# Linformer attention and maxout FFN on one core: attention in four TensorE groups a batch, with projections a batch ahead and AV units in six PSUM banks

## The chip, the core and the metric

The kernel runs on one core of one Trainium2 chip. The metric is the device time of one execution in microseconds (us), lower being better. A core has TensorE (matmuls, with their weight loads on a row of their own), VectorE (DVE), ScalarE (ACT), GpSimd (POOL) and SyncE (SP, which here only issues transfers). TensorE writes to PSUM, of which there are eight banks of 128 partitions by 512 float32 values; VectorE and ScalarE read results out of it.

## The reference

Eight batches of eight heads, 1024 tokens, head dimension 64. Keys and values are first projected along the sequence from 1024 to 64 rows; then comes plain attention, and its output, heads side by side, goes through a maxout layer of three weight matrices and an output matrix.

```python
# q, k, v: (8, 8, 1024, 64)   E, F: (64, 1024)
k_proj = einsum('ks,bhsd->bhkd', E, k)
v_proj = einsum('ks,bhsd->bhkd', F, v)
scores = (q @ k_proj.transpose(0, 1, 3, 2)) / sqrt(64)
scores = scores - max(scores, axis=-1, keepdims=True)
attn = exp(scores)
attn = attn / (sum(attn, axis=-1, keepdims=True) + 1e-09)
x = (attn @ v_proj), heads side by side        # (8192, 512)
h = maximum(maximum(x @ w1, x @ w2), x @ w3)   # w1, w2, w3: (512, 768)
out = h @ w_out                                # (8192, 512), w_out: (768, 512)
```

## The kernel before

The FFN is the dense work. For each half batch (`ch`, 512 tokens) there are 18 first-layer units of four matmuls (`l1`) and, half a batch later, four output units of six (`down`). They take turns in PSUM banks 0 to 3, a ring. After each unit a counter of slots ticks, and at chosen slots a piece of the next batch's attention is put into TensorE's program between dense units. Attention uses banks 4 to 7 (`AB = 4`).

```python
def l1(b, ch, c, jt, i):
    bank = fbank()                                # next of banks 0..3
    for ct in range(NCT):                         # 4 matmuls, 128x512
        nc.tensor.matmul(out=ps[:, bank, :], lhsT=w_sb[i][...], rhs=xT[b % 2][:, ct, ch, :], ...)
    if i == 0:
        nc.scalar.copy(out=h1s[jt % 2], in_=ps[:, bank, :])
    elif i == 1:
        nc.vector.tensor_tensor(out=m12[jt % 2], in0=ps[:, bank, :], in1=h1s[jt % 2], op=ALU.max)
    else:
        nc.vector.tensor_tensor(out=hT[c % 2][:, jt, :], in0=ps[:, bank, :], in1=m12[jt % 2], op=ALU.max)

def down(b, ch, c, tt):
    bank = fbank()
    for jt in range(NJT):                         # 6 matmuls, 128x512
        nc.tensor.matmul(out=ps[:, bank, :], lhsT=hT[c % 2][:, jt, tt * P:(tt + 1) * P], rhs=wo_sb[:, jt, :], ...)
    nc.scalar.copy(out=o[:, tt, :], in_=ps[:, bank, :])
    # ... every second unit: store two of them
```

The attention of batch `b + 1`, placed into the dense work of batch `b`, is six groups on TensorE: `kv`, two of `scores`, `sums` and two of `av`. The array is split into smaller tiles for them, which work side by side: `kv` in two tiles of 128 rows by 64 columns, `scores` in eight of 32 by 64, `sums` and `av` in eight of 64 by 32.

```python
def attention(b, turn):
    i = b % NB                                    # NB = 2
    def kv():                                     # 16 matmuls, bank 4
        for si in range(SI):
            nc.tensor.matmul(out=ps[0:KP, AB, :], lhsT=eT[:, si, :], rhs=k_t[i][:, :, si, :], ...)
            nc.tensor.matmul(out=ps[KP:P, AB, :], lhsT=fT[:, si, :], rhs=v_t[i][:, :, si, :], ...)
        nc.scalar.copy(out=kp2[i][:, :, :, 0, :], in_=kv_k)
        nc.vector.tensor_copy(out=kp_[:, :, 1:], in_=...)      # three more copies of it
        turn(i)                                   # transposing DMA kp2 -> kpT, by SyncE
        nc.scalar.copy(out=vp2[i][KP:P], in_=kv_v[:, 1])
        nc.vector.tensor_copy(out=vp2[i][0:KP], in_=kv_v[:, 0])
    def scores(u):                                # 32 matmuls of 256 columns, banks 4..7
        ...  # lhsT=kpT[i], rhs=qT[i]
        for gg in range(2):
            nc.scalar.activation(out=pT[:, 2 * u + gg]..., in_=ps[:, AB:AB + 4, ...], func=AF.Exp, scale=scale)
    def quads(lhs):                               # 16 matmuls, banks 4..7
        for par in range(2):
            for hh, j, g, u in QUADS:
                nc.tensor.matmul(out=ps[j * HD:(j + 1) * HD, AB + 2 * hh + par, :], lhsT=lhs(rows, g), rhs=pT[rows, g, par, :], ...)
    def sums():
        quads(lambda rows, g: ones[rows, :])
        for u in range(2):
            nc.scalar.activation(out=lns[u], in_=ps[:, AB + 2 * u:AB + 2 * u + 2, :], func=AF.Ln)
    def recip(u):
        nc.scalar.activation(out=rinv[u], in_=lns[u], func=AF.Exp, scale=-1.0)
    def av(half):
        quads(lambda rows, g: vp2[i][rows, g, half, :])
        for u in range(2):
            nc.vector.tensor_tensor(out=xT[b % 2][:, 2 * u + half, :, :], in0=ps[:, AB + 2 * u:AB + 2 * u + 2, :],
                                    in1=rinv[u]..., op=ALU.mult)
    return [(2, kv), (10, lambda: scores(0)), (15, lambda: scores(1)), (20, sums),
            (21, lambda: recip(0)), (22, lambda: recip(1)), (25, lambda: av(0)), (30, lambda: av(1))]
```

In the first batch (`b == 0`), where the pipeline fills and batch 0's own attention is still being finished, the same pieces have slots of their own: `kv` 19, `scores` 27 and 29, `sums` 31, `recip` 32 and 33, `av` 34 and 36. The inputs of batch `b + 2` are loaded by GpSimd from slot 9 of batch `b`, once the transposing DMA has landed (`load_behind_turn`), and `q_flip` transposes its q on VectorE at slots 32 to 38.

Of the kernel before, what the change touches and what calls it, by code (L numbers as in the profile page):

```python
# [10 lines left out]
BF16 = mybir.dt.bfloat16  # L11
# [5 lines left out]
def kernel(ctx: ExitStack, tc: tile.TileContext, q, k, v, E, F, w1, w2, w3, w_out, out):  # L17
# [14 lines left out]
    def T(shape, dt, name):  # L32
        return sb.tile(shape, dt, name=name)
# [77 lines left out]
    AB = 4  # L111
    HD = D // 2

    def attention(b, turn):
        i = b % NB

        def kv():
            for si in range(SI):
                nc.tensor.matmul(out=ps[0:KP, AB, :], lhsT=eT[:, si, :], rhs=k_t[i][:, :, si, :],  # L119
                                 start=(si == 0), stop=(si == SI - 1))  # L120
                nc.tensor.matmul(out=ps[KP:P, AB, :], lhsT=fT[:, si, :], rhs=v_t[i][:, :, si, :],  # L121
                                 start=(si == 0), stop=(si == SI - 1))
            kv_k = ps[0:KP, AB, :].rearrange("p (h dd f) -> p h f dd", dd=HD, f=2)
            kv_v = ps[KP:P, AB, :].rearrange("p (g u dd f) -> p u g f dd", u=2, f=2, dd=HD)
            kp_ = kp2[i].rearrange("k h f r dd -> k (h f) r dd")
            nc.scalar.copy(out=kp2[i][:, :, :, 0, :], in_=kv_k)  # L126
            nc.vector.tensor_copy(out=kp_[:, :, 1:], in_=kp_[:, :, 0:1].to_broadcast([KP, 2 * H, 3, HD]))
            turn(i)
            nc.scalar.copy(out=vp2[i][KP:P], in_=kv_v[:, 1])
            nc.vector.tensor_copy(out=vp2[i][0:KP], in_=kv_v[:, 0])  # L130

        def scores(u):
            for gg in range(2):
                g = 2 * u + gg
                for f in range(2):
                    for r in range(4):
                        rows = slice(r * HD, (r + 1) * HD)
                        for col in range(2):
                            h = HEAD[2 * g + col]
                            nc.tensor.matmul(out=ps[col * KP:(col + 1) * KP, AB + r, gg * 256:(gg + 1) * 256],  # L140
                                             lhsT=kpT[i][rows, h, f, :],
                                             rhs=qT[i][rows, h].rearrange("p (n f) -> p n f", f=2)[:, :, f],
                                             start=(f == 0), stop=(f == 1), tile_position=(r * HD, col * KP))
            for gg in range(2):
                nc.scalar.activation(  # L145
                    out=pT[:, 2 * u + gg].rearrange("p ch (t r n) -> p r (ch t) n", t=4, r=4),
                    in_=ps[:, AB:AB + 4, gg * 256:(gg + 1) * 256].rearrange("p r (si n) -> p r si n", si=SI),
                    func=AF.Exp, scale=scale)

        def quads(lhs):  # L150
            for par in range(2):
                for hh, j, g, u in QUADS:
                    rows = slice(u * KP, (u + 1) * KP)
                    nc.tensor.matmul(out=ps[j * HD:(j + 1) * HD, AB + 2 * hh + par, :],  # L154
                                     lhsT=lhs(rows, g), rhs=pT[rows, g, par, :], start=True, stop=True,
                                     tile_position=(u * KP, j * HD))

        def sums():
            quads(lambda rows, g: ones[rows, :])
            for u in range(2):  # L160
                nc.scalar.activation(out=lns[u], in_=ps[:, AB + 2 * u:AB + 2 * u + 2, :], func=AF.Ln)  # L161

        def recip(u):
            nc.scalar.activation(out=rinv[u], in_=lns[u], func=AF.Exp, scale=-1.0)  # L164

        def av(half):
            quads(lambda rows, g: vp2[i][rows, g, half, :])
            for u in range(2):
                nc.vector.tensor_tensor(out=xT[b % 2][:, 2 * u + half, :, :], in0=ps[:, AB + 2 * u:AB + 2 * u + 2, :],  # L169
                                        in1=rinv[u].rearrange("p (c n) -> p c n", c=2), op=ALU.mult)  # L170

        return [(2, kv), (10, lambda: scores(0)), (15, lambda: scores(1)), (20, sums),
                (21, lambda: recip(0)), (22, lambda: recip(1)), (25, lambda: av(0)), (30, lambda: av(1))]

    def turn_dma(i):
        nc.sync.dma_start_transpose(out=kpT[i].rearrange("p h f k -> p (h f) k"), in_=kp2[i].rearrange("k h f r dd -> k (h f r dd)"))


    state = {"f": 0, "n": 0}
# [53 lines left out]
    def quads0(ch, bank, lhs, hhs=(0, 1)):  # L233
        for hh, j, g, u in QUADS:
            if hh not in hhs:
                continue
            rows = slice(u * KP, (u + 1) * KP)
            nc.tensor.matmul(out=ps[j * HD:(j + 1) * HD, bank + hh, :], lhsT=lhs(rows, g),  # L238
                             rhs=pT[rows, g, ch, :], start=True, stop=True, tile_position=(u * KP, j * HD))

    def k_proj0(g):
        for si in range(SI):
# [16 lines left out]
                             rhs=qT[0][rows, 4 * ch + g, :], start=True, stop=True)  # L259

    def exp0(ch, g, bank):
        nc.scalar.activation(out=pT[:, g, ch, :], in_=ps[:, bank, :], func=AF.Exp, scale=scale)
# [29 lines left out]
    def scores_up0():  # L292
        for g, bank in ((0, 4), (1, 5), (2, 6), (3, 7)):
            scores0(1, g, bank)
        for g in (0, 2):
            nc.scalar.activation(out=pT[:, g:g + 2, 1, :], in_=ps[:, 4 + g:6 + g, :], func=AF.Exp, scale=scale)

    def av_up0():
        for f, bank in enumerate((6, 4)):
# [144 lines left out]

    pend = []
    for b in range(B):
        groups = attention(b + 1, turn_dma) if b + 1 < B else []
        if b == 0:
            g1 = [g for _, g in groups]
            groups = [(9, scores_up0), (12, lambda: sums0(1, 4)), (19, g1[0]),  # L450
                      (21, lambda: q_flip(1, 0)), (22, lambda: q_flip(1, 1)), (24, lambda: q_flip(1, 2)),
                      (25, lambda: q_flip(1, 3)), (27, g1[1]), (29, g1[2]),
                      (31, g1[3]), (32, g1[4]), (33, g1[5]), (34, g1[6]), (36, g1[7])]
        slot = 0
        gi = 0

        def tick():
            nonlocal slot, gi
            slot += 1
            while gi < len(groups) and groups[gi][0] <= slot:  # L460
                groups[gi][1]()
                gi += 1
            if b == 0:
                if slot == 22:
                    load_behind_turn(2, "kvq")
                return
            if b == 1 and slot in (4, 5, 6, 7):
                q_flip(2, slot - 4)
            if b + 2 < B:
                if slot == 9:  # L470
                    load_behind_turn(b + 2)
                if slot in (32, 34, 36, 38):
                    q_flip(b + 2, slot // 2 - 16)

        for ch in range(2):
            c = 2 * b + ch
            if c == 0:
                for part in ((1, range(6), (6, 7, 0, 1, 4, 5)), (2, range(3), (2, 3, 0), q_up0), (2, range(3, 6), (1, 2, 3))):
                    for _ in l1_first(*part):
                        tick()  # L480
                state["f"] = 3
# [51 lines left out]
```

## Time and profile before

| | before |
|---|---|
| time, median of 3 runs | 399.6 us (398.9 to 399.7) |
| span of the profiled execution | 397.2 us |
| TensorE busy | 388.0 us (98%) |
| TensorE weight loads busy | 171.6 us (43%) |
| VectorE busy | 200.0 us (50%) |
| ScalarE busy | 163.7 us (41%) |
| GpSimd busy | 66.6 us (17%) |
| granted TensorE clock | full |

In the profile, PE is TensorE's matmuls, PEld its weight loads, L188 is line 188 of the kernel. A group of instructions is printed as line, engine, operation, written tile <- read tiles, shape, count, then busy time and the mean of one in ns, then the idle time ahead of them and what ended it. Matmuls overlap in the array and their ends are modelled: one dense matmul is shown as 380 ns although the next starts about 216 ns after it. The distance between two starts is therefore the number to read for TensorE, and some records are missing (1043 of 1080 on L188). The lines to know: L188 is the first layer, L212 the output layer, L119 and L121 the k and v projections, L140 the scores, L154 the sums and the AV product, L145 the exponential, L161 and L164 logarithm and reciprocal of the sums, L169 the normalisation.

The chain of work that ended last is made of these shares:

```profile
PE 91%; DMA 5%; issue 1%; ACT 1%; DVE 1%; POOL 0%; POOLq 0%; DVEq 0%
```

### The profile page before, as it was taken

Reading aid. Unit: us, or ns where it says so; the run is one execution under the profiler, and the core shown is the slowest. Engines: PE = TensorE matmul, PEld = TensorE weight load, DVE = VectorE, ACT = ScalarE, POOL = GpSimd, SP = SyncE. Lnnn points to the kernel's source line nnn. Section 1 sums busy time; section 2 is a strip of 40 time slices with the busy share of each in tenths; the row PEclk is TensorE's granted clock in tenths of the full one; section 3 lists DMA queues with packets and bytes.
Section 4 is the critical chain, followed back from the end, with each engine's and each line's share of the span. In section 5 each row is a group of like instructions: output and inputs, shape, how many; then the busy total and the mean of one; then the engine's idle time right before and its main releaser. Section 6 shows DMA issues by size and latency. Waiting matters only on the chain.

```text
span 397.2 us, 6579 instructions
## 1 busy us (share of the span) xinstructions
PE 388.0 (98%) x2686; PEld 171.6 (43%) x2736; DVE 200.0 (50%) x295; ACT 163.7 (41%) x247; POOL 66.6 (17%) x110
## 2 busy tenths in 40 slices
PE   8999999999999999999999999999999999999996
PEld 4444443444444444444444444444444444444443
DVE  3347375654862476434853367433674438433341
ACT  4414447356325632256323662346423472222222
POOL 7452131050004100050001500042000000000000
PEclk9999999999999999999999999999999999999999
DMA  8999989979115972169411991149812111101022
GB/s 222 206 209 206 205 178 203 218 115 203 56 53 101 204 173 80 28 133 206 141 53 31 186 228 62 54 82 196 174 53 76 58 54 53 55 29 77 2 106 106
DMA packets 41293, 48.39 MB, mean 122 GB/s; under 512 B 9136, under 2 KB 36272, under 8 KB 41264
## 3 DMA queue, kind: packets, MB, share of 16 engines
q0 software_dynamic: 31776, 43.52, 53.1%
q1 hardware_dynamic: 8656, 3.54, 4.5%
q10 hardware_dynamic: 832, 0.92, 0.7%
q8 instruction: 21, 0.34, 0.3%
q14 instruction: 8, 0.07, 0.1%
HBM read 57.15 MB, written 16.78 MB: 186 GB/s over the span
## 4 chain that ended last, share of the span: by engine, by line
PE 91%; DMA 5%; issue 1%; ACT 1%; DVE 1%; POOL 0%; POOLq 0%; DVEq 0%
PE ps L188 58%; PE ps L212 19%; PE ps L119 3%; PE ps L154 3%; PE ps L405 3%; DMA w_sb<-in_moe_w_dram 3%; PE ps L140 2%; DMA k_t<-in_k_dram 2%; PE ps L225 1%; PE ps L396 1%; ACT pT L145 1%; DVE xT L169 1%; PE ps L238 0%; PE ps L205 0%; PE ps L285 0%
## 5 line engine op out<-in xcount | busy, mean ns | idle before, releaser
L188 PE MATMUL ps<-xT,w_sb 128*128 128x512 bf16 x1043 | 243.9, 380 | 1.9
L188 PEld LDWEIGHTS <-w_sb 128*128 128x128 bf16 x1080 | 103.1, 98 | 130.9 <-issue 10.2
L193 DVE TENSOR_TENSOR m<-ps,h1s 128x512 f32<-128x512 f32 x90 | 62.1, 690 | 134.3 <-PE ps L188 110.6
L212 PE MATMUL ps<-wo_sb,hT 128*128 128x512 bf16 x348 | 85.0, 380 | 0.5 <-issue 0.2
L191 ACT COPY h1s<-ps 128x512 f32<-128x512 f32 x90 | 52.9, 587 | 67.6 <-PE ps L188 67.6
L214 ACT COPY o_acc<-ps 128x512 f32<-128x512 f32 x59 | 34.6, 586 | 100.6 <-PE ps L212 100.6
L195 DVE TENSOR_TENSOR hT<-ps,m 128x512 bf16<-128x512 f32 x90 | 61.7, 686 | 12.4 <-PE ps L188 5.6
L219 POOL DMA_DIRECT2D out_dram<-o_acc x28 | 15.2, 544 | 273.5 <-ACT o_acc L214 264.6
L212 PEld LDWEIGHTS <-hT 128*128 128x128 bf16 x354 | 33.5, 98 | 43.1 <-issue 4.3
L169 DVE TENSOR_TENSOR xT<-ps,rinv 128x1024 bf16<-128x1024 f32 x28 | 32.9, 1217 | 7.8 <-PE ps L154 7.8
L145 ACT ACTIVATE pT<-ps 128x1024 bf16<-128x1024 f32 x28 | 27.1, 1021 | 16.4 <-PE ps L140 16.3
L99 DVE STREAM_TRANSPOSE qT<-q_t 128x512 f32<-128x512 f32 x28 | 19.4, 695 | 0.0
L87 POOL DMA_DIRECT2D v_t<-in_v_dram x21 | 15.3, 761 | 4.1 <-DMA q_t<-in_q_dram 2.0
L161 ACT ACTIVATE lns<-ps 128x1024 f32<-128x1024 f32 x14 | 13.6, 1021 | 1.6 <-PE ps L154 1.6
L164 ACT ACTIVATE rinv<-lns 128x1024 f32<-128x1024 f32 x14 | 14.2, 1060 | 0.0
L121 PE MATMUL ps<-v_t,fT 128*64 128x512 bf16 x56 | 13.4, 383 | 0.0
L119 PE MATMUL ps<-k_t,eT 128*64 128x512 bf16 x56 | 13.4, 382 | 0.0
L87 POOL DMA_DIRECT2D q_t<-in_q_dram x14 | 10.6, 769 | 3.2 <-DMA wo_sb<-in_moe_w_out_dram 1.1
L87 POOL DMA_DIRECT2D k_t<-in_k_dram x14 | 10.6, 768 | 1.9 <-ACT o_acc L443 1.1
L405 PE MATMUL ps<-xT,w_sb 128*128 128x512 bf16 x46 | 10.6, 380 | 0.2 <-issue 0.2
L126 ACT CAST kp<-ps 64x512 bf16<-64x512 f32 x7 | 4.0, 578 | 15.9 <-PE ps L121 15.9
L306 PE MATMUL ps<-warm 128*128 128x512 bf16 x23 | 8.8, 476 | 1.5 <-DVE ones L338 1.2
(82 smaller groups left out, 155.7 us busy)
## 6 DMA issues: line engine op xcount, KB each, us to landing
out_dram<-o_acc POOLq DMA_DIRECT2D x30, 512.0 KB, 2.9
q_t<-in_q_dram POOLq DMA_DIRECT2D x15, 512.0 KB, 9.3
k_t<-in_k_dram POOLq DMA_DIRECT2D x14, 512.0 KB, 11.8
v_t<-in_v_dram POOLq DMA_DIRECT2D x18, 256.0 KB, 15.2
v_t<-in_v_dram POOLq DMA_DIRECT2D x7, 512.0 KB, 15.0
w_sb<-in_moe_w_dram POOLq DMA_DIRECT2D x4, 384.0 KB, 10.3
k_t<-in_k_dram POOLq DMA_DIRECT2D x4, 256.0 KB, 8.1
w_sb<-in_moe_w_dram POOLq DMA_DIRECT2D x4, 192.0 KB, 10.0
```

Source lines behind the costliest of these rows:

```text
L87: nc.gpsimd.dma_start(out=dst[b % NB][:, slots], in_=sv[:, heads])
L99: nc.vector.transpose(out=qT[b % NB][:, hs].bitcast(FP32).rearrange("p h n -> p (h n)"), in_=q_t[b % NB][:, hs].rearrange("p h si d -> p ( ...
L119: nc.tensor.matmul(out=ps[0:KP, AB, :], lhsT=eT[:, si, :], rhs=k_t[i][:, :, si, :], start=(si == 0), stop=(si == SI - 1))
L145: nc.scalar.activation(out=pT[:, 2 * u + gg].rearrange("p ch (t r n) -> p r (ch t) n", t=4, r=4), in_=ps[:, AB:AB + 4, gg * 256:(gg + 1) * ...
L169: nc.vector.tensor_tensor(out=xT[b % 2][:, 2 * u + half, :, :], in0=ps[:, AB + 2 * u:AB + 2 * u + 2, :], in1=rinv[u].rearrange("p (c n) -> ...
L188: nc.tensor.matmul(out=ps[:, bank, :], lhsT=w_sb[i][:, ct, jt * P:(jt + 1) * P], rhs=xT[b % 2][:, ct, ch, :], start=(ct == 0), stop=(ct == ...
L191: nc.scalar.copy(out=h1s[jt % 2], in_=ps[:, bank, :])
L193: nc.vector.tensor_tensor(out=m12[jt % 2], in0=ps[:, bank, :], in1=h1s[jt % 2], op=ALU.max)
L195: nc.vector.tensor_tensor(out=hT[c % 2][:, jt, :], in0=ps[:, bank, :], in1=m12[jt % 2], op=ALU.max)
L212: nc.tensor.matmul(out=ps[:, bank, :], lhsT=hT[c % 2][:, jt, tt * P:(tt + 1) * P], rhs=wo_sb[:, jt, :], start=(jt == 0), stop=(jt == NJT - 1))
L214: nc.scalar.copy(out=o[:, tt, :], in_=ps[:, bank, :])
L405: nc.tensor.matmul(out=ps[:, bank, :], lhsT=w_sb[i][:, ct, jt * P:(jt + 1) * P], rhs=xT[0][:, ct, 0, :], start=(ct == 0), stop=(ct == NCT ...
```

## The change

The attention of a batch is laid out anew over two batches of dense work, so that it enters TensorE's program at four places instead of six.

- The k, v projection moves one batch ahead: batch `b` computes that of `b + 2`, into a bank of the dense ring, directly before the first scores of `b + 1`. Loads move ahead with it. In the first two batches, where nothing has been projected ahead yet, it keeps places of its own.
- Sums and AV are cut by half batch (`ch`) rather than by pairs of banks. AV has four units (`f`, `ch`) of two banks. Three of them run in one go: one in a pair of ring banks, two in banks 4 to 7; this is `av3`. The fourth, `av1`, is put off into the next batch and takes a pair of ring banks there, directly before the sums of the batch after.
- For this the exponentials `pT` get two buffers and the projected values `vp2` three, and the ring becomes a list from which a pair of neighbouring banks can be taken.

Cut to its core (the old functions stand above; edits by which functions take `b` as an argument, and `pT[0]` in batch 0's own code, are left out):

```diff
-    vp2 = [T([P, NPAIR, 2, D // 2], BF16, f"vp2_{i}") for i in range(NB)]
-    pT = T([P, NPAIR, 2, 512], BF16, "pT")
+    vp2 = [T([P, NPAIR, 2, D // 2], BF16, f"vp2_{i}") for i in range(3)]
+    pT = [T([P, NPAIR, 2, 512], BF16, f"pT{i}") for i in range(2)]
...
+    def kv(b, bank=AB):
...      # the same matmuls, into `bank`; then
+        nc.scalar.copy(out=kp2[i][:, :, :, 0, :], in_=...)
+        nc.scalar.copy(out=vp2[b % 3][KP:P], in_=kv_v[:, 1])
+        nc.vector.tensor_copy(out=kp_[:, :, 1:], in_=...)
+        nc.vector.tensor_copy(out=vp2[b % 3][0:KP], in_=kv_v[:, 0])
+        nc.sync.dma_start_transpose(out=kpT[i]..., in_=kp2[i]...)
...
+    def quads(b, ch, bank, lhs):                 # 8 matmuls, two banks
+        for hh, j, g, u in QUADS:
+            nc.tensor.matmul(out=ps[j * HD:(j + 1) * HD, bank + hh, :], lhsT=lhs(rows, g),
+                             rhs=pT[b % NB][rows, g, ch, :], ...)
+    def sums(b):
+        for ch in range(2):
+            quads(b, ch, AB + 2 * ch, lambda rows, g: ones[rows, :])
+        for ch in range(2):
+            nc.scalar.activation(out=lns[ch], in_=ps[:, AB + 2 * ch:AB + 2 * ch + 2, :], func=AF.Ln)
+    def norm(b, f, ch, bank):
+        nc.vector.tensor_tensor(out=xT[b % 2][:, f::2, ch, :], in0=ps[:, bank:bank + 2, :], in1=rinv[ch]..., op=ALU.mult)
+    def av3(b):
+        lo = fpair()
+        for f, ch, bank in ((0, 0, lo), (1, 0, AB), (0, 1, AB + 2)):
+            av(b, f, ch, bank)
+        norm(b, 0, 0, lo)
+    def av1(b):
+        lo = fpair()
+        av(b, 1, 1, lo)
+        norm(b, 1, 1, lo)
+    ring = [0, 1, 2, 3]
     def fbank():
-        state["f"] = (state["f"] + 1) % 4
-        return state["f"]
+        ring.append(ring.pop(0))
+        return ring[-1]
+    def fpair():
+        for i, j in ((0, 1), (1, 2), (0, 2)):
+            x, y = ring[i], ring[j]
+            if abs(x - y) == 1:
+                ring.remove(x); ring.remove(y); ring.extend((x, y))
+                return min(x, y)
...                                              # slots, with n = b + 1
+        if b == 0:
...          # kv(1) 19, q_flip 21 to 25, load 2 22, scores 27 and 29, sums 31, recip 32 and 33 as before
+            at(35, av3, 1)
+            at(36, norm, 1, 1, 0, AB)
+            at(37, norm, 1, 0, 1, AB + 2)
+        elif b == 1:
+            at(2, kv, 2)
...          # q_flip(2) at 4 to 7
+            at(9, load_behind_turn, 3, "kvq")
+            at(8, scores, 2, 0)
+            at(11, scores, 2, 1)
+            at(15, av1, 1)
+            at(15, sums, 2)
+            at(16, recip, 0)
+            at(18, recip, 1)
...          # at 24: load k, v, q of batch 4
+            at(25, av3, 2)
+            at(26, norm, 2, 1, 0, AB)
+            at(28, norm, 2, 0, 1, AB + 2)
+            at(30, kv, 3)
...          # q_flip(3) at 32 to 38
+        elif n < B:
+            if b + 2 < B:
+                at(3, lambda: kv(b + 2, fbank()))
+            at(3, scores, n, 0)
+            at(8, scores, n, 1)
+            if b + 3 < B:
+                at(11, load_behind_turn, b + 3)
+            at(14, av1, b)
+            at(14, sums, n)
+            at(15, recip, 0)
+            at(17, recip, 1)
+            at(26, av3, n)
+            at(27, norm, n, 1, 0, AB)
+            at(29, norm, n, 0, 1, AB + 2)
...          # q_flip(b + 2) at 33 to 39
+        else:
+            at(5, av1, b)
```

The list is worked off in its order, so in `b == 1` the first scores, which stand behind the load of slot 9, are placed at slot 9.

More of the change, by code (lines that the diff above doesn't have):

```diff
@@ L112 @@
     HD = D // 2
-    def attention(b, turn):
+    def kv(b, bank=AB):
         i = b % NB
[L117 to L173, printed above, removed]
@@ L175, in turn_dma @@
-    def turn_dma(i):
-        nc.sync.dma_start_transpose(out=kpT[i].rearrange("p h f k -> p (h f) k"), in_=kp2[i].rearrange("k h f r dd -> k (h f r dd)"))
-    state = {"f": 0, "n": 0}
-    def fbank():
-        state["f"] = (state["f"] + 1) % 4
-        return state["f"]
+        for si in range(SI):
+            nc.tensor.matmul(out=ps[0:KP, bank, :], lhsT=eT[:, si, :], rhs=k_t[i][:, :, si, :],
+                             start=(si == 0), stop=(si == SI - 1))
+            nc.tensor.matmul(out=ps[KP:P, bank, :], lhsT=fT[:, si, :], rhs=v_t[i][:, :, si, :],
+                             start=(si == 0), stop=(si == SI - 1))
@@ new lines, in kv @@
+        kp_ = kp2[i].rearrange("k h f r dd -> k (h f) r dd")
+        kv_v = ps[KP:P, bank, :].rearrange("p (g u dd f) -> p u g f dd", u=2, f=2, dd=HD)
+        nc.scalar.copy(out=kp2[i][:, :, :, 0, :], in_=ps[0:KP, bank, :].rearrange("p (h dd f) -> p h f dd", dd=HD, f=2))
+        nc.scalar.copy(out=vp2[b % 3][KP:P], in_=kv_v[:, 1])
+        nc.vector.tensor_copy(out=kp_[:, :, 1:], in_=kp_[:, :, 0:1].to_broadcast([KP, 2 * H, 3, HD]))
+        nc.vector.tensor_copy(out=vp2[b % 3][0:KP], in_=kv_v[:, 0])
@@ new lines, in kv, with scores @@
+        nc.sync.dma_start_transpose(out=kpT[i].rearrange("p h f k -> p (h f) k"),
+                                    in_=kp2[i].rearrange("k h f r dd -> k (h f r dd)"))
+    def scores(b, u):
+        i = b % NB
+        for gg in range(2):
+            g = 2 * u + gg
+            for f in range(2):
+                for r in range(4):
+                    rows = slice(r * HD, (r + 1) * HD)
+                    for col in range(2):
+                        h = HEAD[2 * g + col]
+                        nc.tensor.matmul(out=ps[col * KP:(col + 1) * KP, AB + r, gg * 256:(gg + 1) * 256],
+                                         lhsT=kpT[i][rows, h, f, :],
+                                         rhs=qT[i][rows, h].rearrange("p (n f) -> p n f", f=2)[:, :, f],
+                                         start=(f == 0), stop=(f == 1), tile_position=(r * HD, col * KP))
+        for gg in range(2):
+            nc.scalar.activation(
+                out=pT[i][:, 2 * u + gg].rearrange("p ch (t r n) -> p r (ch t) n", t=4, r=4),
+                in_=ps[:, AB:AB + 4, gg * 256:(gg + 1) * 256].rearrange("p r (si n) -> p r si n", si=SI),
+                func=AF.Exp, scale=scale)
@@ new lines, in quads @@
+    def quads(b, ch, bank, lhs):
+        for hh, j, g, u in QUADS:
+            rows = slice(u * KP, (u + 1) * KP)
+            nc.tensor.matmul(out=ps[j * HD:(j + 1) * HD, bank + hh, :], lhsT=lhs(rows, g),
+                             rhs=pT[b % NB][rows, g, ch, :], start=True, stop=True, tile_position=(u * KP, j * HD))
+    def sums(b):
[3 more added lines that the diff above has]
+            nc.scalar.activation(out=lns[ch], in_=ps[:, AB + 2 * ch:AB + 2 * ch + 2, :], func=AF.Ln)
@@ new lines, in recip, with av @@
+    def recip(ch):
+        nc.scalar.activation(out=rinv[ch], in_=lns[ch], func=AF.Exp, scale=-1.0)
+    def av(b, f, ch, bank):
+        quads(b, ch, bank, lambda rows, g: vp2[b % 3][rows, g, f, :])
+    def norm(b, f, ch, bank):
+        nc.vector.tensor_tensor(out=xT[b % 2][:, f::2, ch, :], in0=ps[:, bank:bank + 2, :],
+                                in1=rinv[ch].rearrange("p (u n) -> p u n", u=2), op=ALU.mult)
+    def av3(b):
[3 more added lines that the diff above has]
+        norm(b, 0, 0, lo)
@@ L185, in l1 @@
+    def av1(b):
[3 more added lines that the diff above has]
+    ring = [0, 1, 2, 3]
+    def fbank():
+        ring.append(ring.pop(0))
[4 more added lines that the diff above has]
+            if abs(x - y) == 1:
+                ring.remove(x)
+                ring.remove(y)
+                ring.extend((x, y))
+                return min(x, y)
     def l1(b, ch, c, jt, i):
@@ L238, in quads0 @@
             nc.tensor.matmul(out=ps[j * HD:(j + 1) * HD, bank + hh, :], lhsT=lhs(rows, g),
-                             rhs=pT[rows, g, ch, :], start=True, stop=True, tile_position=(u * KP, j * HD))
+                             rhs=pT[0][rows, g, ch, :], start=True, stop=True, tile_position=(u * KP, j * HD))
     def k_proj0(g):
@@ L261, in exp0 @@
     def exp0(ch, g, bank):
-        nc.scalar.activation(out=pT[:, g, ch, :], in_=ps[:, bank, :], func=AF.Exp, scale=scale)
+        nc.scalar.activation(out=pT[0][:, g, ch, :], in_=ps[:, bank, :], func=AF.Exp, scale=scale)
     def sums0(ch, bank):
@@ L295, in scores_up0 @@
         for g in (0, 2):
-            nc.scalar.activation(out=pT[:, g:g + 2, 1, :], in_=ps[:, 4 + g:6 + g, :], func=AF.Exp, scale=scale)
+            nc.scalar.activation(out=pT[0][:, g:g + 2, 1, :], in_=ps[:, 4 + g:6 + g, :], func=AF.Exp, scale=scale)
     def av_up0():
@@ L446, with at @@
     for b in range(B):
-        groups = attention(b + 1, turn_dma) if b + 1 < B else []
+        n = b + 1
+        groups = []
+        def at(slot, f, *args):
+            groups.append((slot, lambda: f(*args)))
         if b == 0:
[L449 to L453, printed above, removed]
+            at(9, scores_up0)
+            at(12, sums0, 1, 4)
+            at(19, kv, 1)
+            for g, x in enumerate((21, 22, 24, 25)):
+                at(x, q_flip, 1, g)
+            at(22, load_behind_turn, 2, "kvq")
+            at(27, scores, 1, 0)
+            at(29, scores, 1, 1)
+            at(31, sums, 1)
+            at(32, recip, 0)
+            at(33, recip, 1)
+            at(35, av3, 1)
[3 more added lines that the diff above has]
+            at(2, kv, 2)
+            for g in range(4):
+                at(4 + g, q_flip, 2, g)
+            at(9, load_behind_turn, 3, "kvq")
[5 more added lines that the diff above has]
+            at(18, recip, 1)
+            at(24, load, 4, k, k_t)
+            at(24, load, 4, v, v_t)
+            at(24, load, 4, q, q_t)
+            at(25, av3, 2)
+            at(26, norm, 2, 1, 0, AB)
+            at(28, norm, 2, 0, 1, AB + 2)
+            at(30, kv, 3)
+            for g in range(4):
+                at(32 + 2 * g, q_flip, 3, g)
+        elif n < B:
[12 more added lines that the diff above has]
+            at(29, norm, n, 0, 1, AB + 2)
+            if b + 2 < B:
+                for g in range(4):
+                    at(33 + 2 * g, q_flip, b + 2, g)
+        else:
+            at(5, av1, b)
@@ L462, in tick @@
                 gi += 1
[L463 to L473, printed above, removed]
         for ch in range(2):
@@ L480 @@
                         tick()
-                state["f"] = 3
+                ring[:] = [0, 1, 2, 3]
                 for x in range(2):
```

## The prediction

> **What bounds the kernel now.** I read the page first, for the engine that is never idle, then the timeline of TensorE over one batch, for what its time consists of, then the timeline of all engines in the first batch, for real waits. Busy time by engine and the groups:
>
> ```profile
> PE 388.0 (98%) x2686; PEld 171.6 (43%) x2736; DVE 200.0 (50%) x295; ACT 163.7 (41%) x247; POOL 66.6 (17%) x110
> ...
> L188 PE MATMUL ps<-xT,w_sb 128*128 128x512 bf16 x1043 | 243.9, 380 | 1.9
> ...
> L212 PE MATMUL ps<-wo_sb,hT 128*128 128x512 bf16 x348 | 85.0, 380 | 0.5 <-issue 0.2
> ```
>
> TensorE has work all the time; VectorE and ScalarE are half free. "Busy" does not mean streaming at the full rate, though, so the question is how far each stretch lies above that rate. TensorE's timeline, batch b=2 (columns: start us, us, engine, line, operation, count):
>
> ```profile
> 109.76 5.13 PE L188 MATMUL ps<-xT,w_sb 128*128 128x512 bf16 x23
> 114.82 0.40 PE L119 MATMUL ps<-k_t,eT 128*64 128x512 bf16 x1
> ...
> 116.67 1.04 PE L188 MATMUL ps<-xT,w_sb 128*128 128x512 bf16 x3
> ...
> 118.83 2.75 PE L188 MATMUL ps<-xT,w_sb 128*128 128x512 bf16 x12
> 121.42 1.46 PE L212 MATMUL ps<-wo_sb,hT 128*128 128x512 bf16 x6
> 122.72 1.89 PE L188 MATMUL ps<-xT,w_sb 128*128 128x512 bf16 x8
> 124.54 0.67 PE L140 MATMUL ps<-qT,kpT 32*64 32x256 bf16 x32
> 125.14 1.04 PE L188 MATMUL ps<-xT,w_sb 128*128 128x512 bf16 x3
> 126.01 1.46 PE L212 MATMUL ps<-wo_sb,hT 128*128 128x512 bf16 x6
> ...
> 131.89 3.62 PE L188 MATMUL ps<-xT,w_sb 128*128 128x512 bf16 x16
> 135.43 0.62 PE L154 MATMUL ps<-pT,ones 64*32 64x512 bf16 x16
> 135.99 4.49 PE L188 MATMUL ps<-xT,w_sb 128*128 128x512 bf16 x19
> ...
> 161.59 0.40 PE L119 MATMUL ps<-k_t,eT 128*64 128x512 bf16 x1
> ```
>
> The useful number is the distance between starts, since the ends are modelled and a few records are missing. Dense work: 12 matmuls from 118.83 to 121.42, 2.59 us, 0.216 us each. A period runs from the k, v projection at 114.82 to the next at 161.59: **46.77 us**. At the full rate it would be: dense 144 + 48 = 192 matmuls x 0.216 = 41.47; k, v projection 8 pairs side by side x 0.216 = 1.73; scores 2 x 4 steps of 8 side by side at half length (0.108) = 0.87; sums and the two AV halves 3 x 2 steps x 0.216 = 1.30. Sum 45.37. So **1.40 us a batch is loss**, and these lines show where: at each change of tile shape. Before the scores, 8 dense matmuls take 124.54 - 122.72 = 1.82 instead of 1.73 (+0.09); before the sums, 16 take 3.54 instead of 3.46 (+0.09). Inside and out again: projection 114.82 to 116.67, 1.85 instead of 1.73 (+0.12); scores 0.60 instead of 0.43 (+0.17); sums 0.56 instead of 0.43 (+0.13). The first dense unit after a group is 0.01 long. A group thus costs 0.22 (projection), 0.27 (scores), 0.23 (sums, AV): 0.22 + 2 x 0.27 + 3 x 0.23 = 1.45, which accounts for the 1.40. No other wait is left in a steady batch.
>
> **What the skill says.** "TensorEngine Tiling (Array Packing)", Key Properties: changing the tiling mode, not just the tile, drains TensorE. The trace agrees: +0.09 us at every change, dense to any packed shape and back. "TensorE: Matmul & The Clock Gate", Back-to-back issue gap: N/2.4 + 2.5 ns, an estimate of 216 ns for 512 columns; the trace has 0.216. "Perfetto Trace Analysis", Identifying the Most-Contended Engine: matmul busy share doesn't tell the distance from the roofline; true here, since the 98% hide the loss just counted. The same page, Matmuls: groups should rotate through different PSUM banks so that the evacuation of one overlaps the next; this is the rule that the new bank sharing puts at risk.
>
> **The change, part by part.**
>
> (1) *Last AV unit of b beside the sums of b+1; three AV units together.* Both are 64*32, so there is no switch between them. Groups of this shape before: 3 x 7 = 21. After: sums(1) alone, six of AV + sums (b+1 = 2..7), seven of three units, the last AV unit in b=7 alone: 15. Six fewer x 0.23 = **-1.4 us**. The matmuls themselves stay the same number.
>
> (2) *k, v projection of b+2 directly before the first scores of b+1*, in b=2..5, four times. The shapes differ (128*64, 32*64), so one switch stays inside. Saved: an exit, an entry and a restart (0.09 + 0.09 + 0.01) less the inner switch (0.09) = 0.10; x 4 = **-0.4 us**. Groups in all: 42 before, 32 after.
>
> (3) *First batch.* The one long real wait on the path is before the second AV half, for VectorE's normalisation to free the four banks:
>
> ```profile
> 65.25 0.69 DVE L195 TENSOR_TENSOR hT<-ps,m 128x512 bf16<-128x512 f32 x1
> 65.86 2.35 DVE L169 TENSOR_TENSOR xT<-ps,rinv 128x1024 bf16<-128x1024 f32 x2
> ...
> 67.82 1.05 PE L154 MATMUL ps<-pT,vp 64*32 64x512 bf16 x16
> ...
> 68.93 2.35 DVE L169 TENSOR_TENSOR xT<-ps,rinv 128x1024 bf16<-128x1024 f32 x2 [0.73 <-PE ps L154]
> 69.04 2.54 PE L212 MATMUL ps<-wo_sb,hT 128*128 128x512 bf16 x11 [0.16 <-issue]
> ```
>
> That group holds 1.21 us (67.82 to 69.04; 69.036 - 67.824 before rounding) where another holds 0.56: 0.65 of wait. With six banks it goes: three units have banks of their own and the fourth is put off. But without the AV half at 64.57 the first down unit comes 0.6 earlier, and its sixth matmul needs the hT of 65.25 + 0.69 = 65.94; it would be up at about 64.48 + 5 x 0.216 = 65.56, so 0.4 to 0.5 come back as a wait for VectorE. Net **-0.2 us**. The next batch's first layer needs the two normalisations of its own half only, 2 x 1.2 us beside 3.9 us of down units: covered.
>
> (4) *Second batch, b=1, which has no down units in its first half.* The scores move to ticks 9 and 11. Two dense units (1.73) and the first scores (0.60) lie between, while the exponentials of the first take 1.94 after a start 0.73 behind the scores. The first batch has the same distance and there each second scores group starts 0.30 late (58.60 against 58.30). So **+0.3 us**, new. The transposed projection must have landed by tick 9: in the trace its DMA is issued 1.3 us after the projection ends and lands 3.5 us later, 4.8 in all; seven dense units are 6.05 us. Hidden.
>
> (5) *Loads.* Batch 4's load starts in b=1 at about 97 us, right behind batch 3's. In the trace a piece of 512 KB lands each 2.5 to 2.6 us and a batch's k and v need four of them, so v is there near 110 to 112; the projection that needs it runs at about 115. Hidden, with 3 us to spare.
>
> Sum: 399.6 - 1.4 - 0.4 - 0.2 + 0.3 = 397.9; I take **398.0 us**, -0.4%.
>
> **Rivals.**
>
> *A: a new bank wait in every batch.* The dense ring has four banks. After three AV units two are taken until VectorE has normalised, and the projection takes one until ScalarE and VectorE have copied it. For it: after the AV group only two dense units may run before a taken bank is due, 0.86 us each (or 0.86 + 1.3 with a down unit), and the normalisation takes 1.2. Against: following the ring by hand, the pair taken is always of units finished long enough before. Normalisation starts about 0.3 after the first unit and ends near 1.7 us from the group's start; the bank is due at 0.77 + 1.73 = 2.5. After the projection ScalarE holds 0.58 + 0.37 of copies and 1.94 of exponentials; the projection's bank is due after three units, 3.0 us behind the scores, and is free at 1.7. The scarcest case is an AV unit taking the bank of a first-layer unit finished one unit before: in the like place of this trace its copy starts at 123.78, takes 0.58, and the group after the next unit starts at 124.54, 0.18 us later. If this fails by 0.2 us twice in each of six batches, +2.4 us: 400.3.
>
> *B: the packed switch costs less or more than I read.* If 128*64 to 32*64 needs no drain, four times 0.09 more are saved: 397.6. If the entry into a longer group is worse, the whole gain of part 2 is gone: 398.4.
>
> *C: the early loads or the early transposed projection come late.* A wait of 2 to 4 us once, in b=1 or b=2: 400 to 402. The landings above speak against it.
>
> **Range and chances.** The cores of the estimate are counts of switches (sure) times 0.09 to 0.23 us (measured many times, the same to 0.01). What is loose is the start, some +-0.7 us, and rival A, on the high side only. The three runs before span 0.8 us. Range 396.8 to 399.8. All losses of switches together are 7 x 1.4 = 10 us, and the change takes a fifth of them, so 2% (8 us) cannot be reached by this way: faster by over 2% 0.02; within 2% 0.96; slower by over 2% needs 1.2 us of new wait in each batch: 0.02.
>
> **What would show it.** Right: a steady period, projection to projection, of 46.77 - 0.10 - 0.23 = 46.44 us, TensorE leaving for packed shapes four times in it; AV and sums in one group of 24 matmuls, 3 x 0.216 + 0.13 = 0.77 us from its start to the next dense one; the 0.65 wait before the AV at 67.8 gone; the second scores of b=1 late by 0.3. Wrong: dense units of the ring spaced over 0.216 after a packed group, with VectorE's normalisation or ScalarE's exponentials as releaser (rival A); TensorE waiting for the landing of v or of the transposed k (rival C); an inner step of the joint group other than 0.09 (rival B).

## The result, and the profile after

| | before | after |
|---|---|---|
| time, median | 398.89 us (398.82 to 399.7, 6 runs) | 397.17 us (396.77 to 397.82, 6 runs) |
| ratio after / before | | 0.9954, 95% interval 0.9941 to 0.9967 |
| first projection of batch 1 to the last matmul (starts, profiled run) | 346.37 us | 345.23 us |
| start of that projection | 47.02 us | 46.45 us |

The change makes the kernel faster by 1.7 us, inside the range and 0.8 us below the predicted time. The last two rows are from the timelines: the distance from the first matmul of the projection of batch 1 to the last matmul start of the kernel leaves out the first 47 us, in which both programs hold the same instructions. It shows **1.14 us** where the medians show 1.72.

The page of the changed kernel, busy time and the two dense groups:

```profile
PE 389.3 (98%) x2736; PEld 173.7 (44%) x2736; DVE 200.7 (51%) x295; ACT 163.0 (41%) x247; POOL 66.5 (17%) x109
...
L204 PE MATMUL ps<-xT,w_sb 128*128 128x512 bf16 x1080 | 244.5, 379 | 0.0
...
L228 PE MATMUL ps<-wo_sb,hT 128*128 128x512 bf16 x354 | 85.6, 379 | 0.1
```

The busy time teaches nothing here: TensorE's grew by 1.3 us while the kernel got shorter, because no record is missing in this profile (1080 and 354 against 1043 and 348). The second profile of the kernel before, which is complete too, has 391.4 us. The starts tell more. TensorE's timeline of one batch, b=3 (L117 is the k projection, L139 the scores, L153 AV and sums, L204 and L228 the first and the output layer):

```profile
163.51 0.40 PE L117 MATMUL ps<-k_t,eT 128*64 128x512 bf16 x1
...
165.36 0.66 PE L139 MATMUL ps<-qT,kpT 32*64 32x256 bf16 x32
165.95 1.47 PE L228 MATMUL ps<-wo_sb,hT 128*128 128x512 bf16 x6
...
171.24 0.66 PE L139 MATMUL ps<-qT,kpT 32*64 32x256 bf16 x32
...
177.54 0.41 PE L153 MATMUL ps<-pT,vp 64*32 64x512 bf16 x8
177.77 0.62 PE L153 MATMUL ps<-pT,ones 64*32 64x512 bf16 x16
178.32 1.04 PE L204 MATMUL ps<-xT,w_sb 128*128 128x512 bf16 x4
...
188.26 1.46 PE L228 MATMUL ps<-wo_sb,hT 128*128 128x512 bf16 x6
189.64 0.84 PE L153 MATMUL ps<-pT,vp 64*32 64x512 bf16 x24
190.42 2.76 PE L204 MATMUL ps<-xT,w_sb 128*128 128x512 bf16 x12
...
209.95 0.40 PE L117 MATMUL ps<-k_t,eT 128*64 128x512 bf16 x1
```

TensorE leaves the dense work at four places, and the period, projection to projection, is 209.946 - 163.513 = 46.43 us instead of 46.77. AV and sums (177.54 to 178.32) and three AV units (189.64 to 190.42) take 0.775 each (before rounding): three steps of 0.216 and the 0.13 that such a group costs inside and on the way out. From the projection's start to that of the scores it takes 1.85, as long as it took before from the projection's start to the next dense matmul.

By stage, from one batch's first dense matmul to the next one's (the first row from the projection of batch 1):

| stage | before | after | difference | foreseen by the prediction's terms, as they fall on the stages |
|---|---|---|---|---|
| b=0, from the projection | 24.39 | 23.81 | -0.59 | -0.23 - 0.2 - 0.22 (a unit put off) = -0.65 |
| b=1 | 41.59 | 43.61 | +2.03 | +1.73 (a projection moved in) + 0.3 = +2.03 |
| b=2 | 46.77 | 46.95 | +0.18 | -0.33 |
| b=3, 4, 5 together | 140.32 | 139.30 | -1.02 | 3 x -0.33 = -0.99 |
| b=6 | 46.77 | 44.59 | -2.19 | -1.73 - 0.22 (moved out) - 0.23 = -2.18 |
| b=7, to the last matmul | 46.53 | 46.98 | +0.45 | +0.22 + 0.23 = +0.45 |

The differences sum to -1.14, the terms to -1.67. One row is off: b=2, by 0.51 us. What TensorE waited for there is in the waits of the changed kernel (waiting line <- what ended the wait: us in total, times, longest):

```profile
...
PE ps L139 <- ACT pT L144: 0.5, 2, 0.2
PE ps L139 <- DMA kpT<-kp: 0.4, 1, 0.4
PE ps L153 <- ACT pT L144: 0.2, 1, 0.2
...
```

The second line is new. The chain of work that ended last, around it (start us, us, what):

```profile
104.94 0.59 ACT kp L123
...
105.55 0.56 DVE kp L125
...
106.17 12.71 DMA kpT<-kp
118.88 0.04 issue
118.92 0.66 PE ps L139 x29
```

The transposing DMA of batch 3, issued in b=1, takes 12.71 us to land, and the first scores of b=2 start at 118.92 instead of 118.41 (the projection's last step at 118.10 and the usual 0.31). Two questions remained: whether the gain comes from the switches of tile shape, as predicted, or from the banks and the new places; and whether the DMA is late because of the load of batch 4 that runs beside it.

### The profile page after: what moved, and what is told of

Same layout as the page of the kernel before. It is cut to its first block, busy times and chain, and to the rows that moved or that the text cites. A ratio compares the mean times of both kernels' runs of the same rounds, so it can differ in the third digit from the quotient of the medians.

```text
span 395.5 us, 6630 instructions
## 1 busy us (share of the span) xinstructions
PE 389.3 (98%) x2736; PEld 173.7 (44%) x2736; DVE 200.7 (51%) x295; ACT 163.0 (41%) x247; POOL 66.5 (17%) x109
## 4 chain that ended last, share of the span: by engine, by line
PE 87%; DMA 8%; ACT 2%; DVE 1%; issue 1%; POOL 0%; POOLq 0%; DVEq 0%; SPq 0%
PE ps L204 55%; PE ps L228 19%; DMA kpT<-kp 3%; PE ps L153 3%; PE ps L117 3%; DMA w_sb<-in_moe_w_dram 3%; PE ps L139 2%; PE ps L421 2%; DMA k_t<-in_k_dram 2%; PE ps L241 1%; PE ps L412 1%; ACT pT L144 1%; PE ps L254 0%; PE ps L221 0%; ACT lns L160 0%
## 5 line engine op out<-in xcount | busy, mean ns | idle before, releaser
L204 PE MATMUL ps<-xT,w_sb 128*128 128x512 bf16 x1080 | 244.5, 379 | 0.0
L204 PEld LDWEIGHTS <-w_sb 128*128 128x128 bf16 x1080 | 103.6, 98 | 130.0 <-issue 8.4
L228 PE MATMUL ps<-wo_sb,hT 128*128 128x512 bf16 x354 | 85.6, 379 | 0.1
L228 PEld LDWEIGHTS <-hT 128*128 128x128 bf16 x354 | 34.1, 98 | 42.4 <-issue 1.9
L99 DVE STREAM_TRANSPOSE qT<-q_t 128x512 f32<-128x512 f32 x28 | 18.6, 689 | 0.0
L117 PE MATMUL ps<-k_t,eT 128*64 128x512 bf16 x56 | 13.4, 382 | 0.0
L322 PE MATMUL ps<-warm 128*128 128x512 bf16 x26 | 9.4, 469 | 1.2 <-DVE ones L354 1.2
```

Of the source, the lines that this page charges most:

```text
L99: nc.vector.transpose(out=qT[b % NB][:, hs].bitcast(FP32).rearrange("p h n -> p (h n)"), in_=q_t[b % NB][:, hs].rearrange("p h si d -> p ( ...
L117: nc.tensor.matmul(out=ps[0:KP, bank, :], lhsT=eT[:, si, :], rhs=k_t[i][:, :, si, :], start=(si == 0), stop=(si == SI - 1))
L204: nc.tensor.matmul(out=ps[:, bank, :], lhsT=w_sb[i][:, ct, jt * P:(jt + 1) * P], rhs=xT[b % 2][:, ct, ch, :], start=(ct == 0), stop=(ct == ...
```

## The experiments

All but the last start from the changed kernel. Medians of a few runs swing by some 0.4 us with the first 47 us, and the runs were made in three sets, beside which the kernel before took 398.89 us (the result above), 399.18 (the first four experiments) and 399.22 (the other four). So the second column of the table at the end of this section, from the projection of batch 1 to the last matmul, is the sharper one.

**Projection apart from the first scores**

```diff
-                at(3, lambda: kv(b + 2, fbank()))
+                at(2, lambda: kv(b + 2, fbank()))
```

> Theory (each change of tile shape costs 0.09 us, so the joint group saves an exit, an entry and a restart less one inner switch, 0.10 us): projection and first scores apart again costs +0.3 to +0.4 us against the changed kernel (four batches; in b=2 part of it falls into the wait for the transposed projection). The steady period becomes 46.53 instead of 46.43. Rival (the inner switch is free): +0.7 us, period 46.62. Rival (the early projection brings its gain by its place, not by standing beside the scores): 0.

TensorE's timeline of it in b=4:

```profile
211.54 0.38 PE L117 MATMUL ps<-k_t,eT 128*64 128x512 bf16 x1
...
211.86 1.04 PE L204 MATMUL ps<-xT,w_sb 128*128 128x512 bf16 x4
212.82 0.66 PE L139 MATMUL ps<-qT,kpT 32*64 32x256 bf16 x32
213.42 1.47 PE L228 MATMUL ps<-wo_sb,hT 128*128 128x512 bf16 x6
```

The dense unit between them takes 0.96 from start to start, 0.10 more than its four matmuls. The period is 46.54 instead of 46.43: +0.107, as the theory has it, and against both rivals. The total did not follow. From the projection of batch 1 on it is 345.14, 0.09 *less* than the changed kernel, where +0.3 to +0.4 was expected. The three later batches cost 0.32, but b=2 is 0.37 shorter: the wait of 0.5 for the transposed projection is gone, because the scores are due 0.1 later there and the DMA took 12.35 instead of 12.71 us. One swing of that landing hides what the switches cost.

**Put-off AV unit apart from the sums**

```diff
-            at(15, av1, 1)
+            at(14, av1, 1)
...
-            at(14, av1, b)
+            at(13, av1, b)
```

> Theory (a packed group costs 0.23 us for going in and out, whatever its length): the put-off AV unit one dense unit ahead of the sums instead of beside them, in b=1 to 6, costs 6 x 0.23 = +1.4 us against the changed kernel; steady period 46.66. Rival (the gain of the regrouping is the removed wait for banks and not the switches): about 0.

TensorE's timeline in b=4:

```profile
223.77 0.41 PE L153 MATMUL ps<-pT,vp 64*32 64x512 bf16 x8
224.11 1.04 PE L204 MATMUL ps<-xT,w_sb 128*128 128x512 bf16 x4
225.08 0.63 PE L153 MATMUL ps<-pT,ones 64*32 64x512 bf16 x16
225.64 1.04 PE L204 MATMUL ps<-xT,w_sb 128*128 128x512 bf16 x4
```

From start to start, the AV unit takes 0.34 instead of 0.216, the dense unit behind it 0.97 instead of 0.864, and the sums 0.56 for 0.43: one more way in and out of the packed shape. The period is 46.66, +0.23, as expected. The median is 398.8 us, ratio to before 0.9991 (0.9984 to 0.9997): this one edit takes most of the change's gain away. From the projection on it is 346.12, +0.9 and not the +1.4 expected: six times 0.23, less 0.4 by which the wait in b=2 got shorter.

**q of batch 4 only once the transposed projection has landed**

```diff
-            at(24, load, 4, q, q_t)
...
             at(30, kv, 3)
+            at(30, load_behind_turn, 4, "q")
```

> Theory (in b=1 the transposing DMA of batch 3 shares the DMA engines with the load of batch 4 and so lands 12.7 us after issue instead of 3.5): with q of batch 4 loaded only once it has landed, it lands within 4 to 8 us, TensorE's wait of 0.5 us ahead of the first scores of b=2 goes: -0.5 us against the changed kernel. Rival (the wait comes from the order on SyncE or from VectorE's copies): the landing stays late, 0.

The same place in b=2, TensorE's timeline:

```profile
118.29 0.38 PE L117 MATMUL ps<-k_t,eT 128*64 128x512 bf16 x1
...
118.61 0.66 PE L139 MATMUL ps<-qT,kpT 32*64 32x256 bf16 x32
```

From 118.29 to 118.61 it takes 0.31 (before rounding), the plain switch. Time from issue to landing of the seven transposing DMAs, changed kernel first, then this one:

```profile
DMA to landing us min/median/max: 3.5/3.6/12.7
```

```profile
DMA to landing us min/median/max: 3.5/3.6/5.8
```

The slowest is now 5.8 us, that of batch 3 (issued at 106.36, landed at 112.17). It is issued 3.2 us after the projection's start in both kernels, so neither SyncE's order nor VectorE's copies have moved; the load is what changed. In both, the landing follows the last piece of the load under way by some 2 us: that piece landed at 116.97 in the changed kernel and at 109.88 here. b=2 takes 46.44 and the whole 344.68 from the projection on, 0.55 less, as expected. The median of five runs, 397.31 us, does not show it.

**Second scores of b=1 one unit later**

```diff
-            at(11, scores, 2, 1)
+            at(12, scores, 2, 1)
```

> Theory (the second scores of b=1 wait 0.30 us for the exponentials of the first, which take 2.7 us from the scores' start while two dense units leave only 2.4): three units between them take the wait away, -0.3 us against the changed kernel. Rival (the later exponentials then hold up the sums three units on): the wait moves to the sums, 0. The wait for the transposed projection in b=2 may grow by the same 0.3, as its landing is not moved by this: then also 0 in the total, with the 0.3 seen at the scores.

In the changed kernel:

```profile
80.08 0.66 PE L139 MATMUL ps<-qT,kpT 32*64 32x256 bf16 x32
80.67 1.90 PE L204 MATMUL ps<-xT,w_sb 128*128 128x512 bf16 x8
82.80 0.66 PE L139 MATMUL ps<-qT,kpT 32*64 32x256 bf16 x32 [0.23 <-ACT pT L144]
```

With the edit:

```profile
80.54 0.66 PE L139 MATMUL ps<-qT,kpT 32*64 32x256 bf16 x32
81.13 2.76 PE L204 MATMUL ps<-xT,w_sb 128*128 128x512 bf16 x12
83.83 0.66 PE L139 MATMUL ps<-qT,kpT 32*64 32x256 bf16 x32
```

Eight dense matmuls take 2.13 with the wait for the exponentials in them, 0.40 over their 1.73, of which 0.09 is the switch; twelve take 2.70, 0.11 over their 2.59. The wait of 0.31 is gone and has not moved to the sums. b=1 gets shorter by 0.24 us only: 0.07 comes back after the sums, where the ninth dense matmul starts at 89.69, right after VectorE's normalisation of the put-off AV unit (88.42 to 89.64), 0.28 behind the eighth. By its place and time that is the bank wait of rival A, in small. From the projection on it takes 344.87, 0.37 less, with 0.08 of that from a shorter wait in b=2; the median is 397.01.

**First batch spread**

```diff
-            at(29, scores, 1, 1)
-            at(31, sums, 1)
-            at(32, recip, 0)
-            at(33, recip, 1)
+            at(30, scores, 1, 1)
+            at(33, sums, 1)
+            at(34, recip, 0)
+            at(34, recip, 1)
```

> Theory (in the first batch the second scores and the sums each wait 0.30 us for exponentials that two dense units don't cover, and the first output unit waits 0.24 us for VectorE because the copy it builds on stands behind the logarithms): three units between them and the reciprocals later take all three waits away: -0.6 to -0.8 us against the changed kernel from the projection of batch 1 to the end. Rival (the reciprocals, now 1.1 us later, hold up the normalisation and with it the first layer of b=1): 0 or worse.

From the projection of batch 1 to that of batch 2 it takes 24.74 us, against 25.63 and 25.58 in the two profiles of the changed kernel: -0.85 to -0.89, all three waits. From there to the last matmul it is 344.01, -1.2 in all and more than the 0.6 to 0.8 expected: the wait in b=2 is 0.34 shorter in this run, which was not foreseen. The median is 396.61 us, ratio to before 0.9935 (0.9923 to 0.9947).

**All three together**

> The three edits together (q of batch 4 behind the transposed projection, second scores of b=1 one unit later, first batch spread). Theory (they are waits at different places, none hidden behind another): from the projection of batch 1 to the last matmul -0.55 -0.24 -0.7 = -1.5 us against the changed kernel, 343.7 to 343.9 us of 345.2. Rival (a wait removed early only moves the load's landing against the work): less than -1.

TensorE's waits in it, the whole list:

```profile
PE ps L322 <- DVE ones L354: 1.2, 1, 1.2
```

Of the listed waits (0.15 us and more) only the one at the start of the program is left. From the projection on it takes 343.59, 1.65 less than the changed kernel and a little less than the 343.7 to 343.9 expected, and 396.27 us in the median; ratio to before 0.9935 (0.9922 to 0.9948), beside 0.9961 for the changed kernel on the same chip. It is the fastest from the projection on; in the medians it can't be told from the one before it.

**Both kernels again**

> The changed kernel once more, unchanged. Theory (the time up to the projection of batch 1 swings by some half a us from run to run with the first transfers, and the rest of the program does not): from that projection to the last matmul again 345.2 us to within 0.1; its start anywhere between 46.4 and 47.7. If the shorter start belongs to this kernel, the start is again at 46.4 to 46.6 and the median near 397.2.

> The kernel before once more, unchanged: from the projection of batch 1 to the last matmul again 346.4 us to within 0.1, ratio 1.000. With the run above: the change is worth 1.14 us outside the start; anything beyond it in the medians is from the start.

The changed kernel takes 345.20 from the projection on, which starts at 47.67; its median is 397.52 us, ratio 0.9961 (0.9949 to 0.9973). The kernel before takes 346.57, a little over the 0.1 allowed (0.17 of the 0.20 lies in b=0), and starts at 46.63; its median is 399.06 us, ratio to the other runs of itself 0.9997 (0.9989 to 1.0005). So the short start of the first profile is no property of the changed kernel.

What makes the start of 47.67 late is not the first transfers, as the expectation had it. TensorE's timelines of the changed kernel and of its repeat (L322 are matmuls whose result nothing reads, which fill the time until the first inputs are there; L260 is the first projection of batch 0):

```profile
7.89 1.03 PE L322 MATMUL ps<-warm 128*128 128x512 bf16 x4
8.84 0.44 PE L260 MATMUL ps<-eT,k_t 128*64 128x64 bf16 x16
```

```profile
8.46 1.91 PE L322 MATMUL ps<-warm 128*128 128x512 bf16 x4
10.31 0.57 PE L260 MATMUL ps<-eT,k_t 128*64 128x64 bf16 x16
```

The four filler matmuls take 0.95 us from start to start in the one and 1.85 in the other, where they follow each other by 0.43 instead of 0.216, though k of batch 0 had landed by 8.8 in both. The profile of the projection put apart, which starts at 47.68, shows the same; the other eight do not, and start at 46.45 to 47.02. Why TensorE kept that slower pace then is not shown: the profile's granted clock reads 1.00 in all of them.

| run | start of the projection of batch 1 | from there to the last matmul | a steady period | median |
|---|---|---|---|---|
| before | 47.02 | 346.37 | 46.77 | 398.89 |
| before again | 46.63 | 346.57 | 46.78 | 399.06 |
| after | 46.45 | 345.23 | 46.43 | 397.17 |
| after again | 47.67 | 345.20 | 46.43 | 397.52 |
| projection apart | 47.68 | 345.14 | 46.54 | 397.91 |
| AV unit apart | 46.91 | 346.12 | 46.66 | 398.80 |
| q of batch 4 later | 46.69 | 344.68 | 46.43 | 397.31 |
| scores of b=1 later | 46.96 | 344.87 | 46.43 | 397.01 |
| first batch spread | 46.62 | 344.01 | 46.43 | 396.61 |
| all three | 46.50 | 343.59 | 46.43 | 396.27 |

## Why the prediction was right, and where not

**The switches: right, in number and size.** The predicted period is 46.44, the measured one 46.43. Part 1's 0.23 for each group saved is the 0.23 that the AV unit put apart cost; part 2's 0.10 is the 0.107 of the projection put apart. An inner change from 128*64 to 32*64 costs 0.09 like any other (0.31 from the projection's last step to the scores, against 0.216): rival B is out. This agrees with the Trainium skill, "TensorEngine Tiling (Array Packing)", Key Properties, that a change of the tiling mode drains TensorE; the runs show the time and not the draining itself. One thing has to be added to the prediction's 216 ns: in "TensorE: Matmul & The Clock Gate", Back-to-back issue gap, the skill gives that formula for a matmul by itself and some 131 ns for a sustained stream of weight loads and matmuls at 512 columns. Here such a stream kept 0.216 us throughout.

**Rival A, a bank wait in each batch: did not come.** No wait of TensorE is listed beyond the three lines shown above (the lines left out there belong to the program's start), and none of them is for a bank of the ring. Nor do two dense matmuls anywhere behind the first projection start over 0.24 us apart, but for the one wait in the first batch described below. The margins are as reckoned; the timeline of TensorE and VectorE around the three AV units of b=2:

```profile
143.21 0.84 PE L153 MATMUL ps<-pT,vp 64*32 64x512 bf16 x24
...
143.69 2.36 DVE L169 TENSOR_TENSOR xT<-ps,rinv 128x1024 bf16<-128x1024 f32 x2 [0.98 <-PE ps L153]
143.99 2.76 PE L204 MATMUL ps<-xT,w_sb 128*128 128x512 bf16 x12
```

The first normalisation ends at 143.69 + 1.21 = 144.90. Its bank is due with the ninth of those matmuls, at 143.99 + 8 x 0.216 = 145.72: 0.8 us to spare. The scarcest case, an AV unit that takes the bank of a first-layer unit finished one unit before, is the one put off into b=3, which starts at 177.54. ScalarE's copy of that bank:

```profile
176.79 0.59 ACT L207 COPY h1s<-ps 128x512 f32<-128x512 f32 x1 [0.28 <-PE ps L204]
```

It ends at 177.38, 0.16 us before, where 0.18 was reckoned.

**Part 3, the first batch: right in the sum by luck, both terms mis-sized.** The wait before the second AV half was put at 0.65 us. The chain of the kernel before shows less:

```profile
65.86 2.36 DVE xT L169 x2
68.21 0.04 issue
68.26 0.62 PE ps L154 x15
```

The group's first matmul is at 67.82 and the other fifteen start from 68.26 on: 0.44 of wait. The rest, one dense step of 0.216, is a dense matmul whose record is missing after the group (11 shown on the line that should have 12). The second profile of the kernel before has all twelve: there the group holds 0.99 us (67.60 to 68.59), 0.43 over the 0.56 of the others. The reckoning allowed for missing records in the dense rows and not there. The wait that comes back in exchange, for VectorE's hT, is 0.24 and not 0.4 to 0.5. The timeline of the changed kernel there, VectorE and TensorE:

```profile
63.73 0.69 DVE L209 TENSOR_TENSOR m<-ps,h1s 128x512 f32<-128x512 f32 x1 [2.42 <-ACT h1s L207]
63.96 1.70 PE L228 MATMUL ps<-wo_sb,hT 128*128 128x512 bf16 x6
64.53 0.69 DVE L211 TENSOR_TENSOR hT<-ps,m 128x512 bf16<-128x512 f32 x1
65.59 0.84 PE L153 MATMUL ps<-pT,vp 64*32 64x512 bf16 x24
```

Six matmuls fill 1.63 instead of 1.39 with the switch, because the last of them needs the hT that is ready at 64.53 + 0.69. Net -0.44 + 0.24 = -0.2, the number predicted: two errors of 0.2 cancel.

**Part 4, the second scores of b=1: right.** +0.3 was predicted, 0.31 over the usual switch measured, and 0.24 could be had back.

**Part 5: wrong; rival C came, in small.** The prediction had the load of batch 4 start "at about 97 us", the time of the slot it stands in, and looked only for the landing of k and v. A slot places an instruction in TensorE's order, but GpSimd has a queue of its own and had nothing to wait for: in the changed kernel the first piece of that load is issued at 85.0, right after the last of batch 3's, its last at 97.2, and the DMA engines are busy without a break from some 80.5 to 117. v was there at 109.5, in time. What came late was the transposed projection of batch 3, which the prediction had followed in b=1 but not for the one issued beside that load: 12.7 us from issue to landing instead of the 3.5 reckoned with, and +0.51 us where rival C had 2 to 4. Loading q later removes it, alone and in the three edits together, so the cause is shown. That the transfers share the engines in turns is what the Trainium skill says ("DMA: Bandwidth & Descriptors", Queues, rings and completion order: each engine goes round its queues packet by packet); the runs agree with it but do not show the turns themselves.

**The sum.** Had part 5 been right, the prediction for the part behind the first projection would have been -1.67 + 0.51 = -1.16; measured are -1.14 and, with the repeats, up to -1.37. That the medians show 1.7 and 1.5 and so fall close to the -1.6 predicted is in part luck: 0.2 to 0.6 us of it lie outside the stretch between the two marks, and the first 47 us, in which the change does nothing, end between 46.45 and 47.68 in ten profiles without any order by kernel; the prediction had allowed +-0.7 us for this. Whether a small part of that belongs to the change was not settled; the intervals of the medians, about +-0.5 us, are too wide for it.

## What to carry to other kernels

Where TensorE is busy throughout, count its changes of tile shape and price one from the distance of starts: here 0.09 us each, so that joining two packed groups of one shape is worth 0.23 us and of two shapes 0.10. A piece placed at a slot of one engine's program is not placed in time on another: the load moved ahead here ran as early as its own queue allowed, some 11 us before its slot, and what else uses the DMA engines then (here a small transposing transfer that the next batch waits for) has to be looked up at that time. For effects under half a per cent, compare a stretch between two marks in the trace and not only whole times.

## What the runs showed of the hardware that was not expected

A transposing DMA that landed 3.5 to 3.6 us after its issue with little else under way took 12.3 to 12.7 us beside a stream of loads in pieces of up to 512 KB (six profiles), and 5.8 and 6.3 when the stream ended 3.5 and 4.1 us after its issue. The steady period repeats to 0.01 us between runs and kernels (46.43 in six profiles), while the first 47 us vary by 1.2 us: eight of ten profiles lie within 0.6, with a wait of 0 to 0.63 for a piece of the weights (w_sb) in them, and the other two start later, with matmuls that followed each other by 0.43 us instead of 0.216 between 8 and 10 us.
